# The decoder's V in one transfer per half, omega and the first key blocks on ScalarE's queue, first halves first in every round

## The chip, the cores and the metric

The kernel runs on one core of one Trainium2 chip. What is measured is the device time of one launch, in microseconds, as the median of several runs. One further execution was recorded by the hardware profiler; all views of the trace come from that one.

## What is computed

Attention with random features (8 batches, 8 heads, 576 positions, head size 64, 128 features), and behind it a mixing step over the positions and a two-layer network over the channels:

```python
def phi(x):                                  # x: q or k, times 64 ** -0.25
    proj = np.einsum('bhsd,md->bhsm', x, omega)
    h = proj - np.sum(x * x, axis=-1, keepdims=True) / 2.0
    return np.exp(h - np.max(h, axis=-1, keepdims=True)) / np.sqrt(m)
kv = np.einsum('bhsm,bhsd->bhmd', k_p, v)
z = np.sum(k_p, axis=2)
x = np.einsum('bhsm,bhmd->bhsd', q_p, kv) / (np.einsum('bhsm,bhm->bhs', q_p, z)[..., None] + 1e-06)
# x: (8, 576, 512), heads side by side
u = x + (x.transpose(0, 2, 1) @ U @ V).transpose(0, 2, 1)    # U 576 x 32, V 32 x 576
out = u + np.maximum(u @ w_ch1, 0.0) @ w_ch2                 # 512 x 2048, 2048 x 512
```

`U`, `V`, `w_ch1` and `w_ch2` come as 64-bit floats and are turned into 32-bit ones on the chip.

## The kernel before

**Attention (0 to about 310 us).** The work is cut into 16 units, each two batches by two heads. A round of nine steps takes one unit of keys and one of queries, and step `s` of the program's loop (line 860 on) handles one tile of 128 positions of both. In memory the two parts of a round are called `kt` (the first) and `qt` (the second), whether keys or queries are in them. A part comes in two halves, one batch each, and each half in four block transfers (`blocks`, line 616) on SyncE's queue, SP, which is served in order. Every third step VectorE turns three tiles of a part (`turn`, line 640: `xT<-kt`, `xT<-qt`); the first turn of a round reads the first half alone, the later ones the second half too. ScalarE rounds the turned tile to `xh`, GpSimd takes the rest `xl`, and TensorE multiplies both with omega (`omh`, `oml`) into `p_p`. VectorE takes the peak (`nm`), ScalarE the exponential (`e`, four activations per step), and TensorE uses `e`: for keys it sums `p_kv`, for queries it turns `e` (`p_q`), a copy `eT` goes to VectorE or ScalarE in turns, and `p_n` gets the product. `x` is the attention's output.

**The decoder.** Beside this runs a generator (`decoding`, line 102) that turns 64-bit words into floats, piece by piece: U, then V's first half, V's second half, and then the weights. A piece is loaded into `raw` (two buffers), ScalarE reads it twice (line 141 `wf<-raw`, line 144 `low<-raw`), VectorE works on it in three slots (lines 159, 160, 163), GpSimd adds the parts (line 184). The loop advances it by one slot in two of three steps. V is wanted four times over, in the four quarters of 32 partitions, so `v_jobs` (line 375) loads the same 32 rows four times.

**The front.** Omega comes as `once`; VectorE scales it, TensorE turns it, and `omh` (rounded) and `oml` (rest) are made of it. Until the first tiles are there TensorE multiplies a tile `idle`.

**The mixing of the last batch pair and the first products (about 295 to 425 us).** `mixing` (line 411) splits `x` into `mh` and `ml`, and TensorE multiplies with U and V. Then the network begins: its first matrix product is done by a scheme with seven products of sums of blocks, for chunks of 512 positions. `early` is the first chunk and `guest` the second; the sums and the halves `h`, `l` of each operand are given to VectorE (`VE`) or GpSimd (`G_`) by lists that are written out by hand, and tables such as `BEGIN` and `PACE` say how many steps of the side work are done behind which product.

A scheduler builds each engine's order from the program's order; instructions marked to keep the program's order stay so. Each engine works through its list in order.

## Time and profile before

| | us |
|---|---|
| median of 3 timed runs | 1039.98 |
| lowest, highest | 1036.77, 1040.38 |
| the profiled execution | 1022.2 |
| its span, first to last instruction | 1020.3 |
| TensorE busy in the span | 1002.5 |

The profiled execution is its own run; a sum that is read from its trace is made against 1022.2 and then set against the median. TensorE is the engine that is busy nearly all the time, so a wait of another engine matters where TensorE stands still behind it. The granted clock of TensorE has two levels, 1.2 and 2.4 GHz, which the views write as 0.50 and 1.00.

### The profile page before, as it was taken

The numbers are of one execution on the slowest core, as the hardware profiler recorded it, in microseconds if no ns is written. First come the engines' busy times: TensorE is split into PE (matmuls) and PEld (weight loads), VectorE is DVE, ScalarE is ACT, GpSimd is POOL, SyncE is SP. The second block draws the span as 40 slices with busy tenths as digits, with TensorE's granted clock in tenths as the row PEclk, the third lists the DMA queues.
The fourth block names the chain that finished last, engine by engine and source line by source line (L and its number), as shares of the span: only waits on it lengthen the run. The fifth ranks groups of instructions, "written<-read, shape, count | busy, mean of one in ns | idle before, by whom it ended". The sixth has DMA issues, their size and how long they took to land.

```text
span 1020.3 us, 23875 instructions
## 1 busy us (share of the span) xinstructions
PE 1002.5 (98%) x8497; PEld 980.9 (96%) x8497; DVE 844.5 (83%) x1507; ACT 614.6 (60%) x1483; POOL 516.2 (51%) x453
## 2 busy tenths in 40 slices
PE   8999999999999999999999999999999999999998
PEld 7899999999997999999999999999999999999998
DVE  4699898898899796766567565779999999999995
ACT  5889989989885557446355354665444454454442
POOL 4446966867536353323415314525756646646543
PEclk9899999999999999999999999999999999999999
DMA  7688588587444785888679768874555455455451
GB/s 141 137 164 157 115 197 161 112 188 145 88 105 113 214 202 144 225 243 207 179 204 238 183 178 273 258 234 155 176 169 204 146 176 177 145 176 176 145 177 51
DMA packets 380518, 175.51 MB, mean 172 GB/s; under 512 B 275552, under 2 KB 353376, under 8 KB 375920
## 3 DMA queue, kind: packets, MB, share of 16 engines
q1 hardware_dynamic: 378000, 173.67, 64.3%
q8 instruction: 67, 1.10, 0.5%
q10 hardware_dynamic: 2368, 0.30, 0.2%
q14 instruction: 51, 0.42, 0.1%
q0 software_dynamic: 32, 0.03, 0.0%
HBM read 109.97 MB, written 63.96 MB: 170 GB/s over the span
## 4 chain that ended last, share of the span: by engine, by line
PE 58%; DMA 1%; DVE 0%; issue 0%; ACT 0%; DVEq 0%
PE p_q L1409 10%; PE p_p L1409 10%; PE p_n L1409 7%; PE p_n L1028 7%; PE p_p L1028 5%; PE p_q L1028 5%; PE p_kv L1409 5%; PE p_kv L1028 4%; PE p_m L1028 3%; PE p_m L1409 2%; DMA raw<-in_moe_w_ch_dram 1%; DVE g L1014 0%; DMA g<-g 0%; ACT g L1010 0%; DVE u L1334 0%
## 5 line engine op out<-in xcount | busy, mean ns | idle before, releaser
L786 ACT ACTIVATE e<-p_p,nm 128x128 f32<-128x128 f32 x576 | 166.4, 397 | 24.9 <-DVE nm L779 15.9
L1247 ACT CAST gh<-gs 128x512 fp32r<-128x512 f32 x140 | 86.8, 623 | 150.4 <-DVE gs L1219 82.9
L1219 POOL TENSOR_TENSOR gs<-graw 128x512 f32<-128x512 f32 x66 | 108.5, 1654 | 125.2 <-DMA graw<-g 72.0
L1010 ACT ACTIVATE g<-g 128x512 f32<-128x512 f32 x105 | 66.4, 634 | 148.0 <-DVE g L1014 91.7
L651 POOL TENSOR_TENSOR xl<-xT,xh 128x384 fp32r<-128x384 f32 x96 | 97.5, 1033 | 99.9 <-ACT xh L647 82.8
L1254 DVE TENSOR_TENSOR gl<-gs,gh 128x512 fp32r<-128x512 f32 x140 | 132.9, 955 | 7.7 <-ACT gh L1247 6.8
L779 DVE TENSOR_REDUCE nm<-p_p 128x4 f32<-128x512 f32 x144 | 98.1, 683 | 27.4 <-ACT e L786 10.3
L184 POOL TENSOR_TENSOR wf<-wf,low 128x512 int32<-128x512 int32 (+2 forms) x35 | 44.0, 1257 | 130.0 <-ACT g L1010 71.8
L771 PE MATMUL p_p<-omh,xh 128*128 128x256 f32 x288 | 93.2, 324 | 1.9 <-ACT e L786 1.6
L1334 POOL TENSOR_TENSOR u<-u,p 128x256 f32<-128x256 f32 x72 | 80.9, 1153 | 24.8 <-DVE u L1334 22.4
L1254 DVE TENSOR_TENSOR gl<-graw,gh 128x512 fp32r<-128x512 f32 x107 | 83.1, 800 | 3.1 <-ACT gh L1247 3.1
L772 PE MATMUL p_p<-oml,xh 128*128 128x256 f32 x288 | 81.5, 283 | 0.0
L773 PE MATMUL p_p<-omh,xl 128*128 128x256 f32 x288 | 81.4, 283 | 0.0
L1409 PE MATMUL p_p<-wh,gh 128*128 128x256 f32 x288 | 79.5, 276 | 0.0
L1409 PE MATMUL p_p<-wl,gh 128*128 128x256 f32 x288 | 79.5, 276 | 0.0
L1409 PE MATMUL p_p<-wh,gl 128*128 128x256 f32 x288 | 79.5, 276 | 0.0
L1247 ACT CAST gh<-graw 128x512 fp32r<-128x512 f32 x107 | 63.7, 621 | 25.6 <-PE p_n L1409 4.9
L1409 PE MATMUL p_q<-wh,gl 128*128 128x256 f32 x276 | 76.3, 276 | 0.0
L1409 PE MATMUL p_q<-wh,gh 128*128 128x256 f32 x276 | 76.2, 276 | 0.0
L1409 PE MATMUL p_q<-wl,gh 128*128 128x256 f32 x276 | 76.2, 276 | 0.0
L729 PE MATMUL p_n<-kv,eT 128*128 128x65 f32 x512 | 73.2, 272 | 2.9 <-ACT eT L714 1.9
L729 PEld LDWEIGHTS p_n<-kv,eT 128*128 128x128 f32 x512 | 68.3, 194 | 6.2 <-ACT eT L714 2.4
(291 smaller groups left out, 3935.8 us busy)
## 6 DMA issues: line engine op xcount, KB each, us to landing
g<-g SPq DMA_DIRECT2D x282, 128.0 KB, 2.6
graw<-g SPq DMA_DIRECT2D x35, 1024.0 KB, 5.2
raw<-in_moe_w_ch_dram SPq DMA_DIRECT2D x23, 512.0 KB, 4.7
u_dram<-ut SPq DMA_DIRECT2D x36, 256.0 KB, 2.5
u<-u_dram SPq DMA_DIRECT2D x36, 256.0 KB, 2.6
out_dram<-u SPq DMA_DIRECT2D x36, 256.0 KB, 2.5
kt<-in_k_dram SPq DMA_DIRECT2D x120, 72.0 KB, 2.5
qt<-in_q_dram SPq DMA_DIRECT2D x120, 72.0 KB, 2.5
```

Of the source, the lines that this page charges most:

```text
L651: nc.gpsimd.tensor_tensor(out=self.xl[-1], in0=self.turned, in1=f32(self.xh[-1]), op=ALU.subtract)
L729: nc.tensor.matmul(pn[:, h, :], eT[:, h, :], kv[:, h, s // 5, :], start=True, stop=True)
L771: nc.tensor.matmul(o, part.xh[g][:, ts], oh, start=True, stop=False)
L772: nc.tensor.matmul(o, part.xh[g][:, ts], ol, start=False, stop=False)
L773: nc.tensor.matmul(o, part.xl[g][:, ts], oh, start=False, stop=True)
L779: nc.vector.tensor_reduce(out=self.nm[:, :n], in_=self.pp[:, :n], axis=AX.X, op=ALU.max, negate=True)
L786: nc.scalar.activation(out=self.e[:, j, :], in_=self.pp[:, j, :], func=AF.Exp, bias=self.nm[:, j : j + 1])
L1028: K(nc.tensor.matmul(p[:, f, :], x[:, k, fs], y[:, k, :], start=first, stop=(k == 1 and y is ul), skip_group_check=True,))
L1219: K(engine.tensor_tensor(out=to, in0=self.val[x], in1=self.val[y], op=op))
L1247: K(nc.scalar.copy(out=h, in_=v))
L1254: K(nc.vector.tensor_tensor(out=l, in0=v, in1=f32(h), op=ALU.subtract))
L1409: K(nc.tensor.matmul(acc[bank][:, half, :], x[:, ks], y[:, f, :], start=(now.s == 0 and k == 0 and half == 0 and x is h and y is wh), stop ...
```

## The change

In the decoder, each half of V comes by one transfer whose source is repeated four times, in place of four transfers. In the front, omega goes out on ScalarE's queue as its first transfer, before the four first blocks of `qt` (which stood there before too); the load of the exponential's table moves behind them; `omh` is made by VectorE. In the second group of the first round the turn of `qt` is put behind the peak. In all rounds the first halves of both parts are loaded before their second halves. Of the later work, some operations change between VectorE and GpSimd, and three tables have other numbers.

```diff
-                for j in range(4):
-                    nc.sync.dma_start(
-                        out=raw[j * R : (j + 1) * R].rearrange("r s w -> r (s w)"),
-                        in_=words(V)[:, 2 * c : 2 * c + S],
-                    )
+                rows = words(V)[:, 2 * c : 2 * c + S]
+                nc.sync.dma_start(
+                    out=raw.rearrange("p s w -> p (s w)"), in_=rows.unsqueeze(0).broadcast_to([4, R, S])
+                )
...
     once = mp.tile([P, D], F32, name="once", tag="y", bufs=2)
-    nc.gpsimd.dma_start(out=once, in_=omega)
+    nc.scalar.dma_start(out=once, in_=omega)
+    keys[0].load(0)
+    keys[1].load(0, 4)
+    for p in keys:
+        p.load(1)
     nc.vector.memset(warm, 0.0)
     K(nc.scalar.activation(out=warm, in_=warm, func=AF.Exp))
-    keys[0].load(0)
-    keys[1].load(0, nc.scalar)
-    for p in keys:
-        p.load(1)
...
-        nc.scalar.copy(out=omh[r, j, :], in_=pom[r])
+        nc.vector.tensor_copy(out=omh[r, j, :], in_=pom[r])
...
                 new[0].load(0)
-                if r:
-                    new[0].load(1)
             if t == 1:
                 new.append(Queries(r + last, 1))
                 new[1].load(0)
                 if r == 0:
                     for p in keys[:2]:
                         p.load_values(1, "t")
-                    new[0].load(1)
+                new[0].load(1)
                 new[1].load(1)
...
+        if s == G:
+            for p in steps[s].group(1):
+                p.turn()
...
-            engine = nc.vector if self.g >= EARLY_GROUPS and (0, 1, 0, 1, 0, 1, 0)[i] else self.lows
+            engine = nc.vector if self.g >= EARLY_GROUPS and (0, 1, 0, 0, 0, 1, 0)[i] else self.lows
...
-                rest = nc.vector if last and t not in (0, 1, 2, 3, 4, 5, 6, 7) else nc.gpsimd
+                rest = nc.vector if last and t not in (1, 2, 3, 4, 5, 6, 7) else nc.gpsimd
...
-                0, ahead, first, lows=(VE, VE, G_, G_, G_, G_, G_,), sums=(VE, G_, VE, VE,), temps=lambda: next(aside).rearrange("p (k t) -> p k t", k=2)
+                0, ahead, first, lows=(VE, VE, VE, G_, G_, G_, G_,), sums=(VE, G_, VE, VE,), temps=lambda: next(aside).rearrange("p (k t) -> p k t", k=2)
...
-    guest = prepare(1, next(guest_raws), place=lambda i: w_slot(NG - 1, i + 2), lows=(VE, VE, VE, VE, VE, VE, VE,), pool=tp, sums=(VE, G_, G_, G_,))
+    guest = prepare(1, next(guest_raws), place=lambda i: w_slot(NG - 1, i + 2), lows=(VE, VE, VE, VE, G_, VE, G_,), pool=tp, sums=(G_, G_, G_, G_,))
```

The tables: `BEGIN` has 8 in place of 9 as its fourth entry, `PACE` of units 3, 4 and 5 shifts three steps of side work by a product or two, and one more chore is done behind the fourth product of the opening.

Three places in the engines' orders. The first is SyncE's queue, from V's first half to its second; `raw<-in_moe_V_dram` is V, `x<-in_v_dram` are values of later keys, `kt` and `qt` are the parts of the third round. Before:

```order
L382 DMA raw<-in_moe_V_dram 32x576 x4
L665 DMA x<-in_v_dram 128x4x64 x2
L670 DMA x<-in_v_dram 64x2x64
L665 DMA x<-in_v_dram 128x4x64 x2
L670 DMA x<-in_v_dram 64x2x64
L623 DMA kt<-in_k_dram 32x18x32 x8
L623 DMA qt<-in_q_dram 32x18x32 x8
L382 DMA raw<-in_moe_V_dram 32x576 x4
L665 DMA vt_134<-in_v_dram 128x4x64 x2
```

And now:

```order
L382 DMA raw<-in_moe_V_dram 128x1x576
L664 DMA x<-in_v_dram 128x4x64 x2
L669 DMA x<-in_v_dram 64x2x64
L664 DMA x<-in_v_dram 128x4x64 x2
L669 DMA x<-in_v_dram 64x2x64
L622 DMA kt<-in_k_dram 32x18x32 x4
L622 DMA qt<-in_q_dram 32x18x32 x4
L622 DMA kt<-in_k_dram 32x18x32 x4
L622 DMA qt<-in_q_dram 32x18x32 x4
L382 DMA raw<-in_moe_V_dram 128x1x576
L664 DMA vt_134<-in_v_dram 128x4x64 x2
```

`qt`'s first four blocks stand ahead of `kt`'s last four, and three issues fewer stand ahead of them for each half of V.

The second place is VectorE at the first turn of the third round (`xT<-kt`, `xT<-qt`). Before:

```order
L643 STREAM_TRANSPOSE xT<-kt 128x384
L714 COPY eT<-p_q 128x256
L779 TENSOR_REDUCE nm<-p_p 128x4
L160 TENSOR_SCALAR wf<-wf 128x288
L739 TENSOR_SCALAR rec<-p_n 128x4
L643 STREAM_TRANSPOSE xT<-qt 128x384
L740 RECIPROCAL rec<-rec 128x4
```

And now:

```order
L642 STREAM_TRANSPOSE xT<-kt 128x384
L642 STREAM_TRANSPOSE xT<-qt 128x384
L713 COPY eT<-p_q 128x256
L778 TENSOR_REDUCE nm<-p_p 128x4
L160 TENSOR_SCALAR wf<-wf 128x288
L738 TENSOR_SCALAR rec<-p_n 128x4 x2
L739 RECIPROCAL rec<-rec 128x4 x2
```

The turn of `qt` stands right behind that of `kt`, ahead of the copy and the peak.

The third place is ScalarE where it reads V's second half (`wf<-raw`, `low<-raw`; `sv<-wf` is the first half, ready). Before:

```order
L388 CAST sv<-wf 128x288
L714 COPY eT<-p_q 128x256
L786 ACTIVATE e<-p_p,nm 128x128 x4
L647 CAST xh<-xT 128x384
L397 CAST svm<-sv 128x64
L647 CAST xh<-xT 128x384
L141 ACTIVATE wf<-raw 128x288
L144 ACTIVATE low<-raw 128x288
L786 ACTIVATE e<-p_p,nm 128x128 x8
```

And now:

```order
L387 CAST sv<-wf 128x288
L713 COPY eT<-p_q 128x256
L785 ACTIVATE e<-p_p,nm 128x128 x4
L646 CAST xh<-xT 128x384 x2
L141 ACTIVATE wf<-raw 128x288
L144 ACTIVATE low<-raw 128x288
L396 CAST svm<-sv 128x64
L785 ACTIVATE e<-p_p,nm 128x128 x8
```

The read of V's second half stands one cast sooner, with `svm` and eight activations `e` behind it.

## Rows read from the trace of the kernel before

**Rows 1.** The page: TensorE's busy time and share; its granted clock by slice.

```profile
PE 1002.5 (98%) x8497; PEld 980.9 (96%) x8497; DVE 844.5 (83%) x1507; ACT 614.6 (60%) x1483; POOL 516.2 (51%) x453
...
PEclk9899999999999999999999999999999999999999
```

**Rows 2.** Waits of TensorE, 28 to 52 us: us in total, times, longest.

```profile
PE p_n L729 <- ACT eT L714: 1.2, 1, 1.2
PE p_n L729 <- DVE eT L714: 0.5, 1, 0.5
...
PE p_q L709 <- ACT e L786: 0.2, 1, 0.2
```

**Rows 3.** Timeline of VectorE: start, us, work [idle before it and its releaser].

```profile
36.93 0.57 DVE L643 STREAM_TRANSPOSE xT<-kt 128x384 f32<-128x384 f32 x1
...
42.14 0.58 DVE L643 STREAM_TRANSPOSE xT<-qt 128x384 f32<-128x384 f32 x1 [2.74 <-DMA qt<-in_q_dram]
...
43.23 0.66 DVE L779 TENSOR_REDUCE nm<-p_p 128x4 f32<-128x512 f32 x1
```

**Rows 4.** Busy time by stretch: length, busy us of each engine, clock, DMA share, GB/s.

```profile
44.40:51.20 6.80, 6.28 (x28) 5.91 (x29) 4.47 (x12) 5.37 (x18) 3.54 (x4) 0.50 0.68 146
51.20:58.00 6.80, 6.80 (x64) 6.80 (x63) 6.25 (x14) 5.51 (x20) 1.97 (x2) 1.00 0.74 120
```

**Rows 5.** Timeline of SyncE's queue, 20 to 62 us.

```profile
26.80 1.89 SPq L382 DMA_DIRECT2D raw<-in_moe_V_dram  x4
...
29.89 0.63 SPq L670 DMA_DIRECT2D x<-in_v_dram  x1
...
32.48 5.42 SPq L623 DMA_DIRECT2D kt<-in_k_dram  x8
38.00 4.22 SPq L623 DMA_DIRECT2D qt<-in_q_dram  x8
42.75 1.78 SPq L382 DMA_DIRECT2D raw<-in_moe_V_dram  x4
```

**Rows 6.** Tile `raw`, 40 to 50 us: from issue to landing of V's second half.

```profile
DMA to landing us min/median/max: 2.0/2.1/2.1
```

**Rows 7.** DMA queues, 43.7 to 45.6 us: packets, MB, share of 16 engines.

```profile
q1 hardware_dynamic: 189, 0.30, 63.2%
```

**Rows 8.** Timeline of the front, all engines: omega and the first blocks.

```profile
0.75 0.43 ACTq L623 DMA_DIRECT2D qt<-in_k_dram  x1
...
1.27 0.68 POOL L809 DMA_DIRECT2D once<-in_omega_dram  x1 [0.81 <-POOLq L1460]
...
4.67 0.30 DVE L838 TENSOR_SCALAR om<-once 128x64 f32<-128x64 f32 x2 [2.65 <-DMA once<-in_omega_dram]
```

**Rows 9.** Timeline of ScalarE: its reads of V's first and second half.

```profile
32.84 0.55 ACT L141 ACTIVATE wf<-raw 128x288 f32<-128x288 f32 x1
...
48.22 0.48 ACT L141 ACTIVATE wf<-raw 128x288 f32<-128x288 f32 x1
```

**Rows 10.** Busy time by stretch, last round and first products.

```profile
300.00:320.00 20.00, 17.71 (x123) 14.78 (x122) 18.66 (x47) 14.70 (x40) 12.17 (x10) 1.00 0.34 62
320.00:340.00 20.00, 19.76 (x160) 19.01 (x159) 18.84 (x30) 8.32 (x16) 11.30 (x9) 1.00 0.84 210
360.00:380.00 20.00, 19.07 (x163) 18.87 (x162) 18.84 (x32) 10.70 (x23) 10.46 (x10) 1.00 0.83 204
420.00:440.00 20.00, 19.04 (x165) 18.64 (x164) 16.43 (x23) 8.70 (x15) 12.16 (x10) 1.00 0.87 199
```

**Rows 11.** Groups of GpSimd and VectorE, 318 to 362 us: busy us, mean ns.

```profile
L531 POOL TENSOR_TENSOR ts<-uT,ts 128x512 f32<-128x512 f32 x2 | 2.6, 1299 | 0.1
...
L429 DVE TENSOR_TENSOR ml<-x,mh 128x512 fp32r<-128x512 f32 x1 | 0.8, 785 | 0.0
...
L540 DVE TENSOR_TENSOR ul<-x,uh 128x512 fp32r<-128x512 f32 x1 | 0.7, 677 | 0.0
L531 DVE TENSOR_TENSOR ts<-uT 128x512 f32<-128x512 f32 x1 | 0.7, 673 | 0.0
```

More of the change, by code (lines that the diff above doesn't have):

```diff
@@ L614, in performer_mlp_kernel, with blocks @@
     ))
-    def blocks(src, raw, unit, j, queue=None):
+    def blocks(src, raw, unit, j, aside=0):
         pair, hp = unit
@@ L622, in blocks @@
                 r = h * D + a * BLK
-                (queue or nc.sync).dma_start(
+                (nc.scalar if 2 * h + a < aside else nc.sync).dma_start(
                     out=raw[r : r + BLK, j * S : (j + 1) * S].rearrange("i (b c) -> i b c", c=BLK),
@@ L634, in __init__, with load @@
             self.xh, self.xl = [], []
-        def load(self, j, queue=None):
-            blocks(self.src, self.raw, self.unit, j, queue)
+        def load(self, j, aside=0):
+            blocks(self.src, self.raw, self.unit, j, aside)
         def turn(self):
@@ L912, in performer_mlp_kernel @@
                 p.copy(st.s)
-        for st in at("turn1"):
-            for p in st.group(1):
-                p.turn()
+        if s != G:
+            for st in at("turn1"):
+                for p in st.group(1):
+                    p.turn()
         for st in at("exp1"):
@@ L955, in performer_mlp_kernel @@
             st.peak()
+        if s == G:
+            for p in steps[s].group(1):
+                p.turn()
         for st in at("combine"):
@@ L1091, in performer_mlp_kernel @@
     begun = opening()
-    BEGIN = (3, 5, 6, 9, 11, 13, 14, 16, 17, 18, 19)
+    BEGIN = (3, 5, 6, 8, 11, 13, 14, 16, 17, 18, 19)
     spare = 6
@@ L1139, in performer_mlp_kernel @@
     KEPT = 7
-    PACE = {2: (0, 1, 1, 0, 1, 2, 1), 3: (3, 3, 3, 3, 5, 3, 0), 4: (2, 1, 2, 1, 2, 4, 2), 5: (1, 1, 2, 1, 1, 1, 2)}
+    PACE = {2: (0, 1, 1, 0, 1, 2, 1), 3: (3, 3, 4, 3, 5, 3, 0), 4: (1, 1, 2, 1, 2, 4, 2), 5: (2, 1, 1, 1, 1, 1, 2)}
     def bring(i):
@@ L1170, in performer_mlp_kernel @@
             guest.step()
-        for _ in range((1, 1, 1, 1, 1, 1, 1)[i]):
+        for _ in range((1, 1, 1, 2, 1, 1, 1)[i]):
             chores(1, 0)
```

## The prediction

> **What bounds the kernel now.** I read the page first: TensorE is busy 98% of the span, VectorE 83%, ScalarE 60% [rows 1]. So only time in which TensorE stands still, or runs at the lower of its two clock levels, can be won; the reader should look for those places and for nothing else. The granted clock is at full in every slice of the page but the second [rows 1], so I went there with TensorE's waits between 28 and 52 us: 1.2 us for ScalarE's `eT`, 0.5 us for VectorE's `eT`, 0.2 us for `e`, together 1.9 us [rows 2]. These are late by one common cause, which VectorE's timeline shows: it turned `kt` at 36.93, did small work until 39.4, and then stood 2.74 us until the block transfers of `qt` had landed, at 42.14 [rows 3]. Behind that, TensorE ran from 44.4 to 51.2 us at a granted 0.50, which is the 1.2 GHz level, and was back at 1.00 in the next stretch [rows 4].
>
> Why `qt` was late is in SyncE's timeline: SP issues transfers without a pause, four for V in 1.89 us, eight for `kt` in 5.42, eight for `qt` in 4.22, and four for V's second half at 42.75 [rows 5]. SP's issue time, not the transfers, sets when `qt` arrives.
>
> **What the stall costs.** Idle 1.91 us. In the 6.8 us at half clock TensorE was busy 6.28 us [rows 4]; the same work at 2.4 GHz takes half, so 3.14 us are lost. Together 5.05 us.
>
> **The change, part by part.**
>
> *`qt`'s first half.* In the new order SP issues `kt`'s first four blocks, then `qt`'s first four, then the second halves. `qt`'s first half is moved past four `kt` issues, half of 5.42, so 2.7 us. V's first half is one issue in place of four: a transfer of another form, whose nearest row is one of 0.63 us [rows 5], for 1.89, so 1.3 us (1.4 if it takes 0.47 like one of the four). `qt` lands 4.0 us sooner, at 42.1 - 4.0 = 38.1. VectorE now turns `qt` right after `kt`, which ends at 36.93 + 0.57 = 37.5 [rows 3]. It waits some 0.6 us there instead of 2.74, and takes 0.58 us of work that it would do later anyway. The old wait let 2.74 - 1.91 = 0.8 us pass without a loss on TensorE, so a wait of 0.6 is covered, and the low clock should not come. **Gain: 5.05 us**, bounds 0 and 5.05.
>
> *The start.* Omega goes out at ScalarE's first slot, 0.75, taking 0.43, instead of GpSimd's 1.27, taking 0.68; VectorE waited for it until 4.67 [rows 8]. With the same time in flight that is 0.52 + 0.25 = 0.8 us sooner. `qt`'s first blocks go out one issue (0.43) later, behind it, and the activation table's load after all of these: ScalarE is free then, since its first task, the casts of `omh`, goes to VectorE. So the first tiles come up to 0.8 us sooner. But this saves nothing at the end as long as the next arrival is SP's: `qt` lands at 38.1 however early VectorE asks, since SP's string of issues does not move. The wait of 0.6 just grows to 1.4, 0.6 more than what was covered; a start that is 0.8 ahead has that to give. **Counted as 0**, bounds 0 and +0.8. The turn that is put behind the first peak falls under the same cap.
>
> *V's second half, the new wait.* SP reaches it 1.3 us sooner, at 42.75 - 1.3 = 41.4. The four old transfers landed 2.1 us after their issue [rows 6], and their bytes took 63.2% of sixteen engines over 1.9 us, 19.2 us of engine time [rows 7] (189 packets, nearly all of the bytes V's). Each of the four had a quarter of that, 0.3 us over sixteen engines, so about 1.8 us is fixed. One transfer of all on sixteen engines: 0.2 more to issue, 1.8, and 1.2, so 3.2 us, landing at 44.6. If the copy that repeats its source four times were carried by four engines alone: 0.2 + 1.8 + 4.8 = 6.8 us, landing at 48.2. When is it wanted? ScalarE read it at 48.22, after two casts, 5.0 us after VectorE's peak at 43.23 [rows 3, 9]. That peak comes some 2.5 us sooner now, and the stretch behind it runs at full clock; `svm` now stands behind the read: about 45.3. So the wait is 0 at one bound and 2.9 us at the other. Behind ScalarE's waiting read stand `svm` and eight `e` activations, on which TensorE's `p_kv` and `p_q` and VectorE's next peak hang. I take the middle of the bounds, landing at 46.4: a wait of 1.1, of which 0.8 is covered as above. **Cost 0.5 us with some allowance**, bounds 0 and 5.05 (the whole stall again).
>
> For the first half of V the read came at 32.84 [rows 9], and the transfer is issued at 26.80: it lands at 30.0 or 33.6, at worst 0.8 late, which the cover takes. Queued behind it on SP are the values `x` and `kt`; they move up.
>
> The Trainium skill speaks against this edit (DMA: Bandwidth & Descriptors, section Rules for kernel authors): a transfer whose outermost dimension counts fewer than sixteen, with a leading repeat of its source given as the example, runs on at most that many engines. By it V's halves would have four. No run here shows it yet; by it the sum would take the upper bound just given, and that is the first rival.
>
> *All later rounds.* The first halves come no later than before and the second halves four issues later (2.7 us), while they are wanted three steps on, over 5 us. After 42 us no turn of `kt` or `qt` waited for a transfer. Nothing.
>
> *The last round and the first products.* Between 300 and 440 us TensorE stands 2.29, 0.24, 0.93 and 0.96 us in the four windows that are not full, VectorE being busy 18.66, 18.84, 18.84 and 16.43 of 20 [rows 10]. The new tables take from VectorE one sum and two subtractions of the guest chunk and four small ones, and give it two: `ml` of tile 0 (0.79) and `ul` of product 2 (0.68). GpSimd pays 1.30 for what VectorE does in 0.67 [rows 11], and has idle time there. Loss if both added operations lie on the path: 1.5 us. Gain at best: half of the idle, 2.2 us. **Counted as 0.**
>
> **The sum.** 5.05 - 0.5 = 4.5 us off. The profiled execution took 1022.2 us (span 1020.3), the timed ones 1036.8 to 1040.4 with a median of 1040.0; I apply the difference to the median: **1035.5 us**. The spread of the three, 3.6 us, is near what the low clock costs, so the runs may differ in just that.
>
> **Rivals.**
> 1. *The wait comes back at V.* Four engines carry each half, it lands at 48.2, ScalarE stands 2.9 us, TensorE 2.1, and its clock falls as before: 2.1 + 3.1 = 5.2 lost of 5.05 won, 1040 us. For it: the repeat stands first in the transfer's pattern, and a 2.74 us wait did just this [rows 3, 4]. Against: an engine with little else to do may move V faster than the crowded ones of the row did. Chance 0.22.
> 2. *Slower.* The same late V, but nothing covered: ScalarE is the engine that feeds all of TensorE's work here, and a wait of 2.9 us falls through whole, the clock staying low for two stretches of 6.8 us: 2.9 + 6.3 = 9.2 lost, 4.1 slower, 1044 us. It decides once V lands after about 47.5. Chance 0.09; a loss in the last round adds to it.
> 3. *More is won.* V lands in time, the start's 0.8 survives, and the last round gives 1 to 2 us: 7 to 8 us, 1032.5 us. For it: VectorE is the releaser in that stage and gets lighter. Chance 0.2.
>
> That the change doesn't do what it says I give no share: SP's new order shows the four-and-four.
>
> **How the numbers follow.** Forecast 0.49, rivals 0.22, 0.09 and 0.2. About 0.5%, 5.2 us, is what a measurement of this kernel can tell from no change. Faster by more: most of rival 3 and a third of the forecast, 0.33. Slower by more: 0.08. Same: 0.59. The range reaches from rival 3 over the forecast and the return of the stall to the first part of rival 2: 1031 to 1042 us.
>
> **What would show it.** Right: VectorE's wait before `xT<-qt` near 37.5 us is under 1.5 us; no stretch at 0.50 after 44 us; ScalarE's `wf<-raw` of 288 columns waits for V by about 1 us or less; V's landing 3 to 7 us after issue. Wrong: a wait of over 2 us there and a low clock behind it (rivals 1 and 2); V landing in 3.2 us or less clears the way for rival 3; `ml` or `ul` on VectorE as a releaser of TensorE between 300 and 340 us puts the loss into the last round.

## The result and the profile after

| | before | changed |
|---|---|---|
| median of 20 runs, us | 1027.25 | 1033.28 |
| lowest, highest, us | 1019.29, 1040.38 | 1030.05, 1047.74 |
| profiled execution: span, us | 1020.3 | 1039.0 |

The ratio of the changed kernel to the one before is 1.0089, with a 95% interval of 1.0068 to 1.0110: it is slower by about 0.9%, where the prediction had it faster by 0.4%. The three runs on which the prediction stood (1036.8 to 1040.4) lie at the upper end of what the kernel before does; over 20 runs its median is 13 us lower. That the predicted 1035.5 us lies 2 us from the measured median is thus two errors that cancel, in the base and in the sign. Executions of one and the same kernel differ here by lumps (a last stage that is some 14 us longer, a single VectorE instruction of 5 us; see the last section), so below, traces are set against each other at the same matmul and before the last stage.

Both kernels have the same 8497 matmuls, in an order that differs only between near neighbours (at 144 places in the trace of after). This table, worked out from the traces, gives when the n-th of them starts, as the difference to the trace of before (in us, minus is sooner; in the head, when it starts there):

| kernel | 40 (14.6) | 200 (34.0) | 320 (53.9) | 600 (87.5) | 1000 (138) | 2200 (285) | 3400 (437) | 5400 (665) |
|---|---|---|---|---|---|---|---|---|
| changed | -2.2 | +6.1 | +0.6 | +0.6 | +0.6 | +0.9 | +4.2 | +4.9 |

So the start wins 2.2 us. Then some 8 us are lost before matmul 200; the stall of before at 42 us (5.05 us) falls away, which leaves +0.6; and 3.3 us are lost between 285 and 437 us. The page of after, the row that answers to [rows 1]:

```profile
PE 1014.5 (98%) x8497; PEld 995.2 (96%) x8497; DVE 844.2 (81%) x1504; ACT 614.8 (59%) x1481; POOL 508.3 (49%) x457
...
PEclk9899999999999999999999999999999999999999
```

The second slice is again the only one below full, but for another reason. TensorE's waits of after from 28 to 52 us, against the three of [rows 2]; then SyncE's queue, against [rows 5]; then ScalarE's reads of V's first and second half, against [rows 9]:

```profile
PE p_kv L682 <- DMA x<-in_v_dram: 5.9, 1, 5.9
```

```profile
26.79 0.65 SPq L382 DMA_DIRECT2D raw<-in_moe_V_dram  x1
27.55 0.93 SPq L664 DMA_DIRECT2D x<-in_v_dram  x2
28.57 0.75 SPq L669 DMA_DIRECT2D x<-in_v_dram  x1
29.37 3.17 SPq L664 DMA_DIRECT2D x<-in_v_dram  x2
32.58 2.12 SPq L669 DMA_DIRECT2D x<-in_v_dram  x1
34.80 2.16 SPq L622 DMA_DIRECT2D kt<-in_k_dram  x4
```

```profile
34.47 0.46 ACT L141 ACTIVATE wf<-raw 128x288 f32<-128x288 f32 x1 [2.60 <-DMA raw<-in_moe_V_dram]
...
50.73 0.51 ACT L141 ACTIVATE wf<-raw 128x288 f32<-128x288 f32 x1
```

V's first half goes out at 26.79 in one issue, as forecast, but is readable only at 34.47, 7.7 us later. The values `x` behind it are late too: the first of them landed at 35.48, where it landed at 31.17 before. SP hangs 3.17 us at two of the `x` and 2.12 at the next, where it took 1.15 and 0.63 before, and `kt` goes out at 34.80, not 32.48. The DMA view shows what the queue did; first after, 28.2 to 33.6 us, then before, 27.9 to 30.0 (last number of the lower lines: median us from issue to landing):

```profile
q1 hardware_dynamic: 1796, 0.71, 55.7%
...
x<-in_v_dram SPq DMA_DIRECT2D x3, 128.0 KB, 7.7
```

```profile
q1 hardware_dynamic: 416, 0.35, 68.2%
...
x<-in_v_dram SPq DMA_DIRECT2D x2, 128.0 KB, 2.9
```

V's 128 packets of 2304 bytes need the same work in both traces, 18.5 us of engine time before and 17.6 after. Before, the packets ran within 2.05 us, so on nine engines at a time; after, within 5.3 us, on 3.3 at a time. The landings agree: each of the four transfers of before is reported by sixteen updates of its semaphore, the one transfer of after by five, of which four come at its end (33.42 to 34.45 us). And `x` lands 7.7 us after its issue instead of 2.9.

VectorE's turns, against [rows 3], come without a wait (42.80 and 43.29), so the stall of before is gone. `om<-once`, against [rows 8], comes 1.8 us sooner:

```profile
2.84 0.30 DVE L837 TENSOR_SCALAR om<-once 128x64 f32<-128x64 f32 x2 [0.84 <-DMA once<-in_omega_dram]
...
42.80 0.57 DVE L642 STREAM_TRANSPOSE xT<-kt 128x384 f32<-128x384 f32 x1
43.29 0.54 DVE L642 STREAM_TRANSPOSE xT<-qt 128x384 f32<-128x384 f32 x1
```

The stretches that answer to [rows 4] and [rows 10], with the same columns, and TensorE's waits from 296 to 430 us:

```profile
33.56:40.39 6.83, 4.77 (x23) 4.80 (x24) 1.24 (x5) 2.35 (x7) 1.15 (x2) 0.50 0.69 116
40.39:47.20 6.81, 6.77 (x61) 6.54 (x61) 6.10 (x18) 5.86 (x20) 3.52 (x4) 1.00 0.67 128
300.00:320.00 20.00, 16.74 (x123) 14.57 (x121) 18.86 (x48) 14.15 (x41) 10.61 (x9) 1.00 0.30 54
320.00:340.00 20.00, 19.95 (x148) 19.42 (x149) 18.61 (x31) 9.04 (x17) 9.70 (x8) 0.91 0.82 208
360.00:380.00 20.00, 16.29 (x125) 15.93 (x124) 15.09 (x27) 9.87 (x20) 8.37 (x9) 0.91 0.77 181
```

```profile
PE p_kv L1029 <- DVE g L1015: 3.7, 1, 3.7
PE ph L441 <- DVE ut L449: 2.0, 1, 2.0
```

The low clock begins at 33.6 us now, not at 44.4: TensorE still stands for `x` then. In it TensorE was busy 4.77 us, of which half, 2.4, is lost; with the idle 5.88 that makes 8.3 us. The wait for `ut` (at 316) is new and that for `g` (at 371) has grown, each with 3.4 us at 0.50 behind it, which the 0.91 shows; before, the longest wait there was one of 0.9 us, for `g`.

### The profile page after: what moved, and what is told of

Read it like the earlier page. It is cut to its first block, busy times and chain, and to the rows that moved or that the text cites. A ratio compares the mean times of both kernels' runs of the same rounds, so it can differ in the third digit from the quotient of the medians.

```text
span 1039.0 us, 23864 instructions
## 1 busy us (share of the span) xinstructions
PE 1014.5 (98%) x8497; PEld 995.2 (96%) x8497; DVE 844.2 (81%) x1504; ACT 614.8 (59%) x1481; POOL 508.3 (49%) x457
## 4 chain that ended last, share of the span: by engine, by line
PE 60%; DVE 2%; DMA 2%; issue 1%; ACT 1%; SPq 0%; DVEq 0%; ACTq 0%
PE p_p L1410 10%; PE p_q L1410 9%; PE p_n L1410 7%; PE p_n L1029 7%; PE p_p L1029 6%; PE p_q L1029 6%; PE p_kv L1410 5%; PE p_kv L1029 4%; PE p_m L1029 4%; PE p_m L1410 2%; DMA g<-g 1%; DVE g L1015 1%; DMA graw<-g 0%; DMA uraw<-u_dram 0%; SPq L1005 0%
## 5 line engine op out<-in xcount | busy, mean ns | idle before, releaser
L1220 POOL TENSOR_TENSOR gs<-graw 128x512 f32<-128x512 f32 x66 | 100.6, 1528 | 142.8 <-DMA graw<-g 66.7
L1255 DVE TENSOR_TENSOR gl<-gs,gh 128x512 fp32r<-128x512 f32 x140 | 135.1, 972 | 15.5 <-ACT gh L1248 13.7
L1335 POOL TENSOR_TENSOR u<-u,p 128x256 f32<-128x256 f32 x72 | 76.9, 1096 | 32.7 <-DVE u L1335 30.1
L1255 DVE TENSOR_TENSOR gl<-graw,gh 128x512 fp32r<-128x512 f32 x107 | 80.3, 765 | 7.2 <-ACT gh L1248 6.0
```

What stands on the lines that cost most here:

```text
L1220: K(engine.tensor_tensor(out=to, in0=self.val[x], in1=self.val[y], op=op))
L1255: K(nc.vector.tensor_tensor(out=l, in0=v, in1=f32(h), op=ALU.subtract))
```

## The experiments

Two theories stood at first. **A:** V's repeated transfer is carried by few DMA engines, lands late, and holds up what stands behind it. **B:** the loss is in the later work. All ratios are to the kernel before, with their 95% interval. Only those of e1, e6, e8 and e9 lie clear of 1; what the other runs win or lose at a place is read from one trace each. The places in time come from the table, continued (us, minus is sooner than before):

| kernel | 40 | 200 | 320 | 600 | 1000 | 2200 | 3400 | 5400 |
|---|---|---|---|---|---|---|---|---|
| e1: changed, V by four | -2.0 | +0.4 | -3.5 | +2.4 | +7.7 | +7.7 | +11.2 | +12.7 |
| e2: before, V by one | -0.1 | +6.2 | +2.7 | +2.7 | +2.6 | +2.7 | +1.8 | +2.6 |
| e3: changed, later work old | -1.8 | +5.6 | +2.0 | +2.1 | +2.1 | +3.1 | +1.9 | +1.5 |
| e4: both undone | -2.6 | -0.3 | -2.9 | +0.2 | -0.1 | -0.1 | -2.0 | -1.6 |
| e5: e4, second half by one | -2.5 | -0.5 | +1.6 | +2.0 | +2.0 | +2.0 | +0.8 | +1.3 |
| e6: before, later work new | -0.2 | +0.8 | +1.0 | +1.0 | +6.0 | +7.1 | +12.4 | +13.0 |
| e7: e3, V on ScalarE's queue | +0.3 | +3.7 | +2.0 | +2.0 | +7.2 | +8.2 | +6.3 | +7.5 |
| e8: e4, V and weights by GpSimd | -1.8 | -0.5 | -3.8 | -3.0 | +3.6 | +12.2 | +21.0 | +23.2 |
| e9: e4, the lists new | -2.1 | -0.3 | -4.3 | +0.5 | +4.7 | +4.6 | +7.6 | +9.7 |
| e10: e4, the tables new | -1.8 | +0.2 | -3.9 | +2.0 | +1.7 | +1.6 | +3.2 | +5.4 |
| e11: e4, a piece of weights first | -2.2 | -0.5 | -3.7 | -3.7 | -3.7 | -3.7 | -5.0 | -4.6 |
| e12: before, the start alone | -2.0 | -0.6 | -4.1 | -0.3 | +4.6 | +4.7 | +3.3 | +4.5 |
| e13: e11, early chunk new | -2.3 | -0.2 | -4.0 | -4.1 | -4.1 | -4.0 | -4.0 | -2.6 |
| e14: e11, guest chunk new | -2.6 | -0.1 | -3.8 | -1.9 | -1.8 | -1.7 | -1.1 | +0.7 |

The step of 4 to 5 us between matmul 600 and 1000 in e1, e6, e7, e9 and e12 is one VectorE instruction and does not belong to the edits (last section).

### e1, V by four transfers

```diff
-                rows = words(V)[:, 2 * c : 2 * c + S]
-                nc.sync.dma_start(
-                    out=raw.rearrange("p s w -> p (s w)"), in_=rows.unsqueeze(0).broadcast_to([4, R, S])
-                )
+                for j in range(4):
+                    nc.sync.dma_start(
+                        out=raw[j * R : (j + 1) * R].rearrange("r s w -> r (s w)"),
+                        in_=words(V)[:, 2 * c : 2 * c + S],
+                    )
```

> The changed kernel with one part undone: each half of V comes by four transfers again. Theory A (the transfer that repeats its source is carried by few DMA engines, lands late, and the values x behind it land late too; this costs some 8 us around 30 to 40 us): the 5.9 us wait of TensorE for x at 35.6 us and the 6.8 us at a granted 0.50 from 33.6 us are gone, ScalarE's read of V's first half waits under 0.5 us, and the time falls by 8 us, to 1025 us, ratio to before 0.993 to 1.001. Theory B (the loss sits in the late part, between 300 and 430 us, by the new tables): the time falls by at most 3 us, ratio 1.006 to 1.009. Either way no wait over 1.5 us for qt near 38 us should be there, since SP then still issues the first halves first.

Ratio 1.0073 [1.0036, 1.0111]. TensorE's longest wait from 28 to 52 us:

```profile
PE p_kv L683 <- DMA x<-in_v_dram: 1.0, 1, 1.0
```

The 5.9 us are 1.0, the low clock there is gone, and e1 is 3.5 us ahead of before at matmul 320, as theory A wanted. But the whole time fell by far less than 8 us: by matmul 600 the lead is a lag of 2.4, and the waits for `ut` and `g` are there. So A holds for the front, B for the later part, and something in between was foreseen by neither.

### e2, before with V by one transfer

The edit of e1 turned round, in the kernel before.

> The kernel before with one edit alone: each half of V by one transfer that repeats its source. Theory A: V's first half lands 6 us and more after its issue, values x behind it 5 to 8 us after theirs (2.7 before), TensorE stands 4 to 6 us before 36 us with a stretch at 0.50 behind it. The kernel before has its own stall of 5 us at 42 us, which goes only if the later start of everything covers it: ratio 1.003 to 1.008. Theory B: one issue less for each row, V not late in effect: ratio 0.996 to 1.001.

Ratio 1.0034 [0.9996, 1.0072]. The wait for `x` comes with this one edit (the view of TensorE's waits, 28 to 52 us; 3.4 us, under the 4 to 6 expected), and the clock is low from 35.7 us for 6.8 us:

```profile
PE p_kv L682 <- DMA x<-in_v_dram: 3.4, 1, 3.4
```

It costs 6.2 us at matmul 200; the own stall of before then falls away (a later front needs `qt` later), which leaves 2.7. That is A, in the trace; the ratio's interval just reaches 1.

### e3 and e4, the later work as before, with V by one and by four

The ends of two of the lines:

```diff
-(0, 1, 0, 0, 0, 1, 0)[i] else self.lows
+(0, 1, 0, 1, 0, 1, 0)[i] else self.lows
...
-lows=(VE, VE, VE, VE, G_, VE, G_,), pool=tp, sums=(G_, G_, G_, G_,)
+lows=(VE, VE, VE, VE, VE, VE, VE,), pool=tp, sums=(VE, G_, G_, G_,)
```

and likewise the other five edits of lists and tables; e4 has e1's edit on top.

> The changed kernel with the later work as before: the seven edits of lists and tables (operand halves, early and guest chunk, the rest of tile 0, the begin, pace and chore tables) are undone; front, order of loads and V stay changed. Theory A alone (the late part neither wins nor loses): same as the changed kernel, ratio to before 1.007 to 1.011, the 5.9 us wait for x still there. Theory B (late tables lose 4 us): ratio 1.004 to 1.006, no wait of over 1 us between 300 and 380 us and no stretch at 0.50 there.

> The changed kernel with both undone, V by four transfers and the later work as before: left are omega on ScalarE's queue, the casts and turns of the front, and first halves first. If Theory A and B both hold: 12 us under the changed kernel, 1021 us, ratio 0.992 to 0.996, faster than before. If only A holds: equal to the run with V alone undone. If only B holds: equal to the run with the later work undone. If first halves first is itself what loses: ratio over 1.004 with neither the wait for x nor the late waits.

Ratios 1.0041 [0.9999, 1.0082] and 1.0039 [0.9990, 1.0088]. In e3 TensorE stands 4.0 us before the same `p_kv`. The view names ScalarE's read of V as what ended that wait, but `p_kv` reads `e` and `x`, and the first `x` landed at 34.64, 0.13 us before it. The wait for `ut` is gone and that for `g` is back to 0.9, and from matmul 2200 to 3400 e3 gains 1.1 us where the changed kernel loses 3.3. So B's share is about 4.5 us. e4 was to reach 1021 us and be clearly faster. By the ratio it is not; its lowest time is where it was to be. The lowest times of the kernels follow the traces: 1030.05 us changed, 1026.17 in e1, 1024.55 in e3, 1021.67 in e4 and 1020.56 before, where the first is of 20 runs, the last of 35 and the others are of 12. In its trace e4 is 2.9 us ahead at matmul 320 and has nothing left at 600. ScalarE's timeline of e4 shows where it went, with the matching place of e11 (below) under it:

```profile
77.42 0.66 ACT L141 ACTIVATE wf<-raw 128x512 f32<-128x512 f32 x1 [1.37 <-DMA raw<-in_moe_w_ch_dram]
```

```profile
75.07 0.70 ACT L141 ACTIVATE wf<-raw 128x512 f32<-128x512 f32 x1
```

A piece of the weights stands on SP behind the round's sixteen block transfers. It goes out at 72.5 us in e4 and 71.7 before, so no sooner, but is wanted 2.9 us sooner. Behind it wait ScalarE's `eT` and TensorE (1.7 us, with 3.4 us at 0.50).

### e5, V's second half alone by one transfer

```diff
-                nc.sync.dma_start(
-                    out=raw.rearrange("p s w -> p (s w)"), in_=rows.unsqueeze(0).broadcast_to([4, R, S])
-                )
+                if c:
+                    nc.sync.dma_start(
+                        out=raw.rearrange("p s w -> p (s w)"), in_=rows.unsqueeze(0).broadcast_to([4, R, S])
+                    )
+                else:
+                    for j in range(4):
+                        nc.sync.dma_start(out=raw[j * R : (j + 1) * R].rearrange("r s w -> r (s w)"), in_=rows)
```

and the later work as before.

> The changed kernel with the later work as before and V's first half by four transfers; only V's second half comes by one. Theory A1 (it is the first half alone that hurts, since the values x are queued right behind it and wanted 3 us later): equal to the run with V by four transfers and the later work as before, 1021 to 1026 us, no wait of TensorE over 1.5 us before 40 us, and no wait of ScalarE for V's second half over 0.5 us. Theory A2 (both halves hurt alike): a new wait of 2 to 3 us behind the second half near 48 us, 3 to 5 us slower than that run.

Ratio 1.0031 [0.9983, 1.0079]. In the trace A2 holds, with a longer wait than expected; the ratio, beside e4's 1.0039, doesn't show it. ScalarE's timeline:

```profile
45.26 0.95 ACT L650 CAST xh<-xT 128x384 fp32r<-128x384 f32 x2
50.50 0.46 ACT L141 ACTIVATE wf<-raw 128x288 f32<-128x288 f32 x1 [4.29 <-DMA raw<-in_moe_V_dram]
```

V's second half, issued at 42.7, is readable at 50.5. TensorE stands 4.2 us, then runs 6.8 us at 0.50; against e4, 4.5 us are lost at matmul 320. This is the wait of which the prediction spoke. In the changed kernel the first half's lateness hides it: ScalarE reaches the second at 50.73 there, and it had landed at 50.17.

### e7, V's one transfer on ScalarE's queue

```diff
-                nc.sync.dma_start(
+                nc.scalar.dma_start(
                     out=raw.rearrange("p s w -> p (s w)"), in_=rows.unsqueeze(0).broadcast_to([4, R, S])
```

> The changed kernel with the later work as before, V's one transfer for each half issued by ScalarE instead of SyncE. If V's own lateness is the cost (few engines carry it): its 128 packets still take about 5 us, ScalarE still waits 1.5 to 2.6 us for it, TensorE still stands 3 us or more near 32 to 35 us, time as with V on SyncE's queue, 1024 to 1029 us. If it is what is queued behind it (the values x and SyncE's further issues): x lands 2.5 to 3.5 us after issue again, SyncE has no issue of over 1 us there, TensorE's wait for x goes, and the time falls by 3 us to 1021 to 1026 us.

Ratio 1.0032 [0.9990, 1.0073]. On that queue both halves go out much earlier than they are read, the first at 4.2 us, the second at 37.2 and read at 52.3, so nobody waits for V itself, and `x` is in time. The second is alone on its queue; the DMA view from 38.7 to 43.3 us, and SP's issues beside the first and the second half:

```profile
q10 hardware_dynamic: 131, 0.29, 23.5%
```

```profile
5.67 5.64 SPq L622 DMA_DIRECT2D qt<-in_k_dram  x4
```

```profile
38.83 5.38 SPq L622 DMA_DIRECT2D kt<-in_k_dram  x4
```

23.5% of sixteen engines is 3.8 engines, over 4.6 us. So V is slow by itself, and four engines are what it gets. And beside each half four issues on the other queue took over 5 us, which take 2.1 elsewhere. Their landings are late too: the blocks that SP issued from 37.2 to 40.6 us landed 4.8 to 6.3 us after their issue, those just before and behind them 2.1 to 2.4. Beside the first, that made `kt` late by 4.8 us at 11.6 us: TensorE stood 2.7 us and ran 10 us at 0.50 (+3.7 at matmul 80), and the wait for `qt` near 44 us came back (3.1 us). So neither expectation is met: it isn't V's own landing, and not only what stands behind it on its own queue, but the transfers of another queue as well. What holds those the traces don't name; that each of them has a share on the four engines which V occupies would fit, and isn't shown. A single transfer with another order of its source's dimensions is untested.

### e6, before with the later work new

> The kernel before with the seven edits of the later work alone. Theory B (they put VectorE's tile ut behind the early sums, and the stores of g behind the loads of u): TensorE waits 2.0 us for ut near 316 us and 3 to 4 us for g near 371 us, each with a stretch of 3.4 us at a granted 0.50 behind it; 4 to 5.5 us slower than before, ratio 1.004 to 1.006. Rival (those waits came from the late front, that is from the state in which the attention reaches 300 us): neither wait, ratio 0.998 to 1.002.

Ratio 1.0052 [1.0003, 1.0101]. TensorE's waits, 296 to 430 us:

```profile
PE p_kv L1028 <- DVE g L1014: 4.7, 1, 4.7
PE ph L442 <- DVE ut L450: 2.0, 1, 2.0
```

From matmul 2200 to 3400 5.3 us are lost (3.3 in the changed kernel, 3.4 in e1; in the seven traces with the lists and tables as before, e8 left aside, 1.0 to 1.9 are gained there). B holds, and it needs nothing of the new front.

### e9 and e10, the lists and the tables apart

e9 is e4 with the four edits that move operations between VectorE and GpSimd; e10 is e4 with `BEGIN`, `PACE` and the chores.

> The changed kernel with V by four transfers, and of the seven edits of the later work only the four that move operations between VectorE and GpSimd; the begin, pace and chore tables are as before. Theory L (the lists make the loss: VectorE gets one more halving of the early chunk, and the sums of the guest go to GpSimd): TensorE waits 2.0 us for ut near 315 us and about 3 us or more for g near 372 us, 4 to 5 us slower than the run with the later work as before. Theory T (the tables make it): neither wait. Mixed: the wait for ut is here and that for g is in the other run, 2 to 4 us each with the clock.

> The changed kernel with V by four transfers, and of the seven edits of the later work only the three tables (begin, pace, chores). Theory L: no wait for ut, no wait over 1.2 us for g near 372 us, time of the run with the later work as before. Theory T: both waits, 4 to 5 us slower. Mixed: only the wait for g near 372 us, since the tables decide how many loads of u stand ahead of the stores of g on SyncE.

Ratios 1.0116 [1.0063, 1.0170] and 1.0042 [0.9998, 1.0085]. Waits of e9, then the longest of e10, 296 to 430 us:

```profile
PE p_kv L1030 <- DVE g L1016: 2.8, 1, 2.8
PE ph L442 <- DVE ut L450: 2.0, 1, 2.0
```

```profile
PE p_kv L1030 <- DVE g L1016: 1.3, 1, 1.3
```

Both long waits come with the lists. Against e4, which gains 1.9 us over that stretch, the lists lose 4.9 (e9) and the tables 3.4 (e10), the latter in small waits only, without a stretch at 0.50. The two don't add up: together, in e1, they lose 5.3.

### e11, a piece of the weights first

```diff
+                if r == 0:
+                    new[0].load(1)
+                    new[1].load(1)
-                new[0].load(1)
-                new[1].load(1)
...
             advance(decoder)
+        if 0 < r and r + 1 < NR and t == 1:
+            for p in rounds[r + 1]:
+                p.load(1)
```

> The changed kernel with V by four transfers, the later work as before, and one piece of the weights put ahead of eight block transfers in SyncE's queue, at 66 instead of 72.5 us; nothing else moves. If the front's gain of 2.9 us was lost to that piece: ScalarE's wait of 1.4 us at 77 us and TensorE's 1.7 us with its stretch at 0.50 are gone, TensorE is 2.5 to 3 us ahead of the kernel before from 58 us to 300 us and 4 to 5 us ahead at 430 us, and the fastest runs are at 1017 to 1019 us, ratio 0.994 to 0.998. If SyncE's string of issues as a whole sets the pace: the wait comes at the next piece or at a block transfer before 100 us, and the gain is gone by then, ratio 0.999 to 1.003.

Ratio 1.0000 [0.9954, 1.0046]. In the trace it did what was hoped. SP's order is e4's but for this one transfer, issued at 67.5 us; nobody waits for it (row above), the lead of 3.7 us stands unchanged from matmul 320 to 2200 and is 5.0 at 3400. So e4's gain was lost to that one piece. In the whole time the gain is not to be seen; the fastest run, 1019.8 us, missed the 1017 to 1019 expected.

### e8, V and the weights issued by GpSimd

```diff
-            nc.sync.dma_start(out=raw.rearrange("p n w -> p (n w)"), in_=words(src))
+            nc.gpsimd.dma_start(out=raw.rearrange("p n w -> p (n w)"), in_=words(src))
```

and V's four likewise.

> The changed kernel with the later work as before, V by four transfers, and V's and the weights' transfers issued by GpSimd instead of SyncE. It tests what takes back the front's gain: with V by four transfers TensorE was 2.9 us ahead of the kernel before at 58 us, and lost it at 79 us, where ScalarE waited 1.4 us for the weights' piece that stands behind a round's block transfers in SyncE's queue. If SyncE's issues set that: no wait for the weights before 100 us, 3 us ahead of the kernel before at 300 us, ratio 0.994 to 0.998. If GpSimd has no time for ten more issues of about 0.7 us each per 100 us, or its transfers land late: waits of TensorE for GpSimd's xl or ml, ratio above 1.000.

Ratio 1.0312 [1.0260, 1.0364], by far the slowest. Up to matmul 600 the lead holds (-3.0), which agrees with e11. Then VectorE and GpSimd get into each other's way, as the last section takes up. The longest VectorE instruction of the stretch, and GpSimd's last before it ends:

```profile
94.48 7.07 DVE L159 TENSOR_SCALAR wf<-wf 128x512 f32<-128x512 f32 x1
```

```profile
100.01 1.25 POOL L429 TENSOR_TENSOR ml<-x,mh 128x512 fp32r<-128x512 f32 x1
```

TensorE stands 4.9 us behind it. GpSimd worked without a gap from 91.6 us or earlier to 101.3, and VectorE's instruction ended 0.3 us after that.

### e12, the start alone

```diff
-    nc.gpsimd.dma_start(out=once, in_=omega)
+    nc.scalar.dma_start(out=once, in_=omega)
...
-        nc.scalar.copy(out=omh[r, j, :], in_=pom[r])
+        nc.vector.tensor_copy(out=omh[r, j, :], in_=pom[r])
```

and the table's load and the turn moved as in the change.

> The kernel before with the start alone: omega on ScalarE's queue, the casts of omh on VectorE, the turn behind the first peak; V by four transfers, order of loads and later work as before. If SyncE's issues cap it: TensorE is 2.2 to 2.6 us ahead up to 28 us, VectorE's wait for qt near 42 us grows from 2.7 to 4 to 5 us, and behind it nothing is left, ratio 0.998 to 1.001, end within 1 us of the kernel before in the trace. If it is not capped: 2 us ahead at 300 us, ratio 0.997 to 0.999.

Ratio 1.0000 [0.9956, 1.0044]. From 22 to 48 us SP's issues stand within about 0.2 us of before, and yet the wait for `qt` at 42 us is gone: VectorE, with the turn behind the peak, does more of its other work first and turns `qt` at 42.47 without a wait. The cap comes one round later:

```profile
57.79 0.58 DVE L643 STREAM_TRANSPOSE xT<-qt 128x384 f32<-128x384 f32 x1 [2.12 <-DMA qt<-in_q_dram]
```

```profile
61.15:67.98 6.83, 6.83 (x36) 6.83 (x35) 4.72 (x14) 5.76 (x19) 2.84 (x4) 0.50 0.96 177
```

A lead of 4.1 us at matmul 320 is 0.3 at 600.

### e13 and e14, the early and the guest chunk apart

e13 is e11 with one more half of the early chunk and the first `ml` on VectorE; e14 is e11 with the guest's and the weights' lists.

> The run with the piece of the weights first, and of the edits of the later work two alone: one more halving of the early chunk (ul of product 2) and ml of the first tile go from GpSimd to VectorE. If VectorE's added 1.5 us are what makes ut late: TensorE waits 1.5 to 2 us for ut near 311 us with a stretch of 3.4 us at a granted 0.50, 2 to 3 us lost between 295 and 345 us against the run with the piece of the weights first; no wait over 1.2 us for g. If not: neither wait, same time.

> The run with the piece of the weights first, and of the edits of the later work two alone: one sum and two halves of the guest chunk, and four small halves of the weights, go from VectorE to GpSimd. If these make g late (GpSimd's slower sums, or the loads of u that they let go ahead of the stores of g): TensorE waits 2.5 to 4 us for g near 367 us with a stretch of 3.4 us at 0.50, 4 to 5 us lost between 345 and 400 us; ut not late, or late by less than 0.5 us. If ut is late here and not in the other run, GpSimd's sums near 312 us are the cause of that too.

Ratios 0.9953 [0.9900, 1.0007] and 1.0011 [0.9954, 1.0067]. TensorE's waits, 290 to 425 us, e13 and then e14:

```profile
PE ph L442 <- DVE ut L450: 2.0, 1, 2.0
```

```profile
PE p_kv L1034 <- DVE g L1020: 2.2, 1, 2.2
```

Each edit has its wait, as expected, and both lose less than expected. From matmul 2200 to 3400, e11 gains 1.2 us, e13 nothing, e14 loses 0.6; between matmul 2700 and 2950 alone e14 loses 2.8. e13 is still slower there than e11, but its median over 10 runs, 1020.72 us, is the lowest of all kernels here. Its interval just reaches 1, so that it beats the kernel before is not shown.

## Why the prediction was wrong

**The step that failed** is the sentence on V's first half: "it lands at 30.0 or 33.6, at worst 0.8 late, which the cover takes. Queued behind it on SP are the values `x` and `kt`; they move up." Issued at 26.79, V landed at 34.45, 0.9 us behind the upper bound; ScalarE waited 2.6 us for it. What failed outright is the last part: `x` did not move up but landed 7.7 us after its issue, and TensorE stood 5.9 us for it. V was priced as if it had the engines to itself; that it would slow what is issued beside it (e7: on another queue too) was put at nothing. That cost 8.3 us in the changed kernel, and 6.2 by the edit alone (e2). What V's own lateness would have cost with `x` in time, no run separates: ScalarE read V only 1.15 us before TensorE had `x`.

**The rule of the Trainium skill** that the prediction weighed (DMA: Bandwidth & Descriptors, section Rules for kernel authors: a leading repeat confines a transfer to at most as many engines as there are copies) agrees with the trace: 3.8 engines in e7. The prediction took the middle between sixteen and four engines for the second half, and for the first it held both bounds to be covered. Rival 2, V late and not covered, with the clock falling behind it, was right in kind, at 0.09, and named the wrong half. That its 9.2 us lie near the 8.3 measured is luck: it has 2.9 of waiting for V and 6.3 of low clock, where 5.9 of waiting for `x` and 2.4 of low clock were measured.

**V's second half**, cost 0.5 with bounds of 0 and 5.05: in the changed kernel nothing, hidden by the first half; by itself 4.5 us (e5), near the upper bound.

**`qt`'s first half**, gain 5.05: the stall went. With V by four, the kernels with the new order win 2.6 to 4.1 us between matmul 200 and 320 (e1, e4, e9 to e11, e13, e14), where the stall of before lies. So the term was right in kind and too large, and e12, which wins 3.5 there with the old order, shows that the order of loads was not needed for it.

**The start**, counted as 0: it gave 2.2 us, not 0.8, at matmul 40, and without V's edit it was used up to a few tenths by matmul 200 (e4: -0.3). That SP's string of issues caps it was right, though the cap bites at 58 us (e12) rather than 42.

**All later rounds**, put at nothing, failed too: a lead of 2.9 us in the front meets the weights' piece at 77 us, which SP issues when it did before. In the changed kernel the front was too late for that to matter; e4 and e11 show it.

**The last round**, counted as 0 with a loss of at most 1.5: measured 3.3 in the trace of after, 5.3 in e6. The two operations added to VectorE were priced by their length. What counted was what then ran side by side. Of the two, `ul` comes behind `ut`, and `ml` takes its 0.68 us some 15 us ahead of it. But the orders of the engines shift with the edits, and one of GpSimd's `ml` now starts just ahead of the last sum that VectorE makes before `ut`, not behind it. After, then before:

```profile
315.02 1.28 POOL L428 TENSOR_TENSOR ml<-x,mh 128x512 fp32r<-128x512 f32 x1 [0.52 <-ACT mh L426]
315.23 1.62 DVE L530 TENSOR_TENSOR x<-x 128x512 f32<-128x512 f32 x1
```

```profile
314.30 0.68 DVE L531 TENSOR_TENSOR x<-x 128x512 f32<-128x512 f32 x1
315.19 1.29 POOL L429 TENSOR_TENSOR ml<-x,mh 128x512 fp32r<-128x512 f32 x1 [1.81 <-ACT mh L427]
```

The sum takes 1.60 to 1.66 us in all five traces with these edits (after, e1, e6, e9, e13) and 0.68 in the ten others, e8 left aside. So `ut` comes later, and TensorE, which gets there sooner in the new order (at 310.7 us in e13, 312.4 in e11), stands 2.0 us for it. The guest's lists make `g` late (2.2 to 4.7 us). In after VectorE waited 3.3 us for the earlier `g` to be stored, and SP had ten loads of `u` ahead of that store, as in all five traces with these lists (after, e1, e6, e9, e14); in the ten others there are seven. No run changes that order alone, so this is argued, not shown. Behind each of the waits the clock was low for 3.4 to 6.8 us.

**The base** of 1040 us was too high; the profiled execution at 1022.2 was nearer to the median of many.

The trace of after adds up to 4.9 us by 665 us; the ratio says about 9. The rest is not explained. Without the 14 us of its last stage this execution would have taken some 1027 us, 3 less than the fastest of the 20, so most executions of the changed kernel lose something that its trace does not have. The VectorE instruction of 5 us (last section) would do; no run shows it for this kernel.

## What to carry to other kernels

Before one transfer replaces several, ask how many engines will carry it (a source repeated four times in front got about four here), and price not only its own landing but also that of all transfers issued while it runs. Where one queue issues without pause, a lead won elsewhere is kept only up to the next transfer whose place on that queue hasn't changed: list its next deliveries and when each is wanted, and move the first one that would be late (e11). An operation moved to another engine costs by what then runs side by side and by what stands behind it, not by its length.

## What the runs showed of the hardware

The same VectorE instruction near 118 us took 1.22 to 1.25 us in eleven of sixteen traces and 5.04 to 5.10 in five, whatever the edit. Line 159 in before and in e6:

```profile
L159 DVE TENSOR_SCALAR wf<-wf x1: 1242/1242/1242, 118.0 to 118.0; 128x512 f32<-128x512 f32 x1
```

```profile
L159 DVE TENSOR_SCALAR wf<-wf x1: 5083/5083/5083, 119.0 to 119.0; 128x512 f32<-128x512 f32 x1
```

In both it ended 0.3 us after an instruction of GpSimd: before, after the one that ran when it started; in e6, after the fifth since it started, the last of a string without a gap that lasted from 109.6 us or earlier to 123.8. In e8 another ended in the same way after 7.07 us. With TensorE idle 3.1 us (e6) and the clock low for 3.4 to 6.8 us behind it, this is a lump of 4 to 5 us in the time. The Trainium skill (SBUF — State Buffer, section SBUF: two separate sides) describes a pair of ports that VectorE and GpSimd share, as an exclusive lock and not a split: a GpSimd instruction, or one of VectorE in a two-port mode or with two inputs in SBUF (the latter only against a GpSimd instruction that reads SBUF), gets it for the whole instruction, whichever starts first, and the other is blocked. The sum of 1.62 us, with two inputs, agrees with that: it ended 0.55 us after GpSimd's `ml`, where it takes 0.68 alone. The instruction of line 159 agrees with a lock, but it waited through five GpSimd instructions, not one; why in five traces and not in the others stays open.

In the last stage the matmuls of some traces follow each other more slowly, at the same granted clock. Before, then after, 680 to 1018 us; the first bracket is TensorE's count:

```profile
680.00:1018.00 338.00, 336.74 (x2972) 336.54 (x2970) 317.52 (x445) 150.91 (x263) 188.47 (x138) 1.00 0.49 164
```

```profile
680.00:1018.00 338.00, 337.43 (x2863) 336.98 (x2862) 313.78 (x433) 152.39 (x265) 173.06 (x133) 1.00 0.49 165
```

That is 4% fewer in the same time, some 14 us over the stage. e3, e7, e8, e9 and e11 show it too, while e1 and e6, with the same later work as after, don't; so it is no effect of the edits, and its cause stays open.
